# Two linear-attention layers and two MLPs on one core: queries between the entry steps, a fixed TensorE order, eps added by TensorE, the last group scaled on GpSimd, activation tables asked for early

## The chip, the core and the metric

The kernel runs on one core of a Trainium2 chip. A core has TensorE (PE: matrix products, written to PSUM), VectorE (DVE), ScalarE (ACT: functions by table, and copies), GpSimd (POOL) and SyncE (SP), whose queue issues the transfers here. Each engine runs its own instructions in order and waits on semaphores of the others. The metric is the device time of one execution in microseconds (us). In the profile PE stands for matmuls and PEld for the loads of their stationary operand.

## The reference

Input `x` is (1, 2048, 576) in bfloat16. Four residual layers follow each other, A, B, A, B, with the same weights for both A and both B. A is linear attention with 32 heads of 18 columns; B is an MLP of 4608 hidden columns.

```python
def _A_ref(x, wqkv, wo):
    qkv = (x @ wqkv) ...                      # q, k, v: 32 heads of 18
    phi = lambda t: jnp.where(t > 0, t + 1, jnp.exp(t)) + 1e-6
    pq, pk = phi(q), phi(k)
    kv = jnp.einsum("bhsd,bhse->bhde", pk, v)
    z = jnp.einsum("bhsd->bhd", pk)
    num = jnp.einsum("bhqd,bhde->bhqe", pq, kv)
    den = jnp.einsum("bhqd,bhd->bhq", pq, z)[..., None] + 1e-6
    o = num / den
    return o... @ wo
def _B_ref(x, w1, b1, w2, b2):
    y = _layernorm(x, axis=-1)
    h = _gelu(jnp.einsum("bsd,df->bsf", y, w1) + b1)
    return jnp.einsum("bsf,fd->bsd", h, w2) + b2
x = x + _A_ref(_layernorm(x), A_wqkv, A_wo)
x = x + _B_ref(_layernorm(x), B_w1, B_b1, B_w2, B_b2)
# the same two lines once more
```

## The kernel before

**Tiling.** The 2048 tokens are 16 tiles of 128 (`NT`), or four chunks of 512 (`NCA`, `CA`; four tiles a chunk, `TPC`). The 576 columns are five pieces of 128 rows for a product (`KD`), and the 32 heads five groups of 7, 7, 7, 7 and 4 heads (`G`, `GR` rows: 126, or 72 for the last). `yT` holds the normalised input, transposed.

**An attention layer** (`layer_A`; layers 0 and 2). A loop over the 16 tiles makes keys and values (`kv_proj`, L325, L333, L336: key halves in a `ps_h` buffer each, values in a PSUM pair) and adds the tile's outer products to `kvacc` (`kv_acc`, L349). `phi_from_psum` is two ScalarE passes (Exp L278, Identity L280) and two VectorE passes (L281, L283) for each key half or query block. `q_proj(g, c)` (L355) makes the queries of one group and chunk, 126 or 72 rows by 512 tokens, into `pq[(g, c)]`; ten of the twenty stand in this loop.

What I call the entry follows. VectorE masks `kvacc` into `kvT` (L372, L376); five tiny products give `z` (L382), and `zsel` (L384, L386) spreads it. `den_stage(c)` makes the denominators of a chunk for all heads (L409, 20 small matmuls), adds 1e-6 on VectorE (L413), takes the reciprocal (L416) and spreads it into `quad_rden` (L418). `kv_wo(g)` (L394) multiplies a group's key-value matrix by its rows of `wo`; the result is cast from PSUM by ScalarE for even and VectorE for odd groups (L399, L401). `scale_stage(g, c)` brings the reciprocals to the rows of a group (L424), copies them to SBUF on ScalarE (`rden_bc`, L426) and multiplies `pq` by them on VectorE (L427). Before, the next five queries (chunk 2) then come in one block, and `den_stage(1)`.

The output loop over 16 tiles has `wo_stage(t)`: ten matmuls into a PSUM pair (L435; two pairs, `accA` and `accB`, take turns; for each half the groups 0 to 4 in order), `residual` (L305: PSUM plus the old `x`, on VectorE, then a store), and between them the `scale_stage` calls for the next chunk, the last five queries and the other two `den_stage` calls. `prefetch_xo` loads the old `x` of the next tiles with three buffers (L290, L293; for a following MLP with `b2` added on GpSimd, L295). The first four output tiles are normalised at once for the MLP (`LNPipe`: statistics on VectorE, L223 to L231, the root on GpSimd, L236, the normalisation, L248 on ScalarE or L252, and the transposes, L261); later tiles are stored and loaded again (`xl`, L218).

**An MLP layer** (`LayerB`; 1 and 3): per chunk nine groups of four 128-column blocks into PSUM (`m1_group`, L526), Gelu on ScalarE (`hT`, L522; tiny copies `relay_sb`, L531, order the matmuls), and then four tiles of 72 matmuls (L571) and the residual.

**What sets the order.** The program is written for a scheduler that keeps the data dependences and orders each engine's instructions by program order and by its own planned times; it can pull later, ready work ahead, across layers too. An edge of kind `NOSYNC` fixes an order without a semaphore. The helper `pe` chains matmuls that way:

```python
def pe(inst):
    if pe_chain["on"]:
        if pe_chain["last"] is not None:
            tc.add_manual_dep(inst.ins, pe_chain["last"], NOSYNC, reason="TensorE order in the MLP")
        pe_chain["last"] = inst.ins.name
    return inst
```

Before, the chain is on in the MLPs only. The PSUM buffers for short products (`ps_h`) are three, used in turn by keys, queries, `z`, denominators, `rden_ps` and the MLP's `h_ps`. Most SBUF blocks (`pk`, `pq`, `kvwo`, `rden_bc`, `quad_rden`, `hT`) come from one pool, `blk`, of 36.

Of the kernel before, what the change touches and what calls it, by code (L numbers as in the profile page):

```python
# [15 lines left out]
P = 128  # L16
NT = S // P
KD = 5
# [17 lines left out]
def build(tc, A_x, A_wqkv, A_wo, B_w1, B_b1, B_w2, B_b2, out, dbg=None, n_layers=4):  # L36
    nc = tc.nc
    dbg = dbg or {}
    with ExitStack() as ctx:
# [23 lines left out]
        z_row = const.tile([P, 1], BF16, name="z_row")  # L63

        def build_masks():
            sel = nc.gpsimd.affine_select
            nc.gpsimd.memset(maskz[:], 1.0)
            sel(out=maskz[:], in_=maskz[:], compare_op=ALU.is_ge, fill=0.0,
                base=0, pattern=[[-DH, 7], [0, DH]], channel_multiplier=1)
            sel(out=maskz[:], in_=maskz[:], compare_op=ALU.is_ge, fill=0.0,  # L70
                base=DH - 1, pattern=[[DH, 7], [0, DH]], channel_multiplier=-1)
            sel(out=maskz[:], in_=maskz[:], compare_op=ALU.not_equal, fill=1.0,
                base=-126, pattern=[[0, 7], [0, DH]], channel_multiplier=1)
            nc.gpsimd.memset(z_row[:], 0.0)
            sel(out=z_row[:], in_=z_row[:], compare_op=ALU.not_equal, fill=1.0,
                base=-126, pattern=[[0, 1]], channel_multiplier=1)
            nc.gpsimd.memset(head_sel[:], 1.0)
            sel(out=head_sel[:], in_=head_sel[:], compare_op=ALU.is_ge, fill=0.0,
                base=0, pattern=[[126, G], [-DH, H]], channel_multiplier=1)
            sel(out=head_sel[:], in_=head_sel[:], compare_op=ALU.is_ge, fill=0.0,  # L80
                base=DH - 1, pattern=[[-126, G], [DH, H]], channel_multiplier=-1)
            nc.gpsimd.memset(quad_mask[:], 1.0)
            sel(out=quad_mask[:], in_=quad_mask[:], compare_op=ALU.is_ge, fill=0.0,
                base=0, pattern=[[-32, 4], [0, P]], channel_multiplier=1)
            sel(out=quad_mask[:], in_=quad_mask[:], compare_op=ALU.is_ge, fill=0.0,
                base=31, pattern=[[32, 4], [0, P]], channel_multiplier=-1)
            nc.gpsimd.memset(head_bc[:], 0.0)
            hb = head_bc[:, :, 0:126].rearrange("p g (h d) -> p g h d", h=7)
            for quad in range(4):
                sel(out=hb, in_=hb, compare_op=ALU.not_equal, fill=1.0,  # L90
                    base=-32 * quad, pattern=[[-7, G], [-1, 7], [0, DH]], channel_multiplier=1)
# [182 lines left out]
        lnp = LNPipe()  # L274

        def phi_from_psum(ps_ap, out_ap, rows, n):
            e = work.tile([P, 512], BF16, name="phi_e", bufs=3)
            nc.scalar.activation(out=e[0:rows, 0:n], in_=ps_ap, func=ACT.Exp)  # L278
# [34 lines left out]
        def layer_A(li, next_kind, pre_a1=None):  # L313
# [5 lines left out]
            def kv_proj(t):  # L319
                tok = slice(t * P, (t + 1) * P)  # L320
                pk = blk.tile([P, D], BF16, name="pk", tag="blk")
                for half in range(2):
                    kp = ps_h.tile([P, 512], F32, name="k_ps", tag="h")
                    for k in range(KD):
                        nc.tensor.matmul(kp[:, 0:HALF], lhsT=yT[:, k, tok],  # L325
                                         rhs=wqkv_sb[:, k, D + half * HALF: D + (half + 1) * HALF],
                                         start=(k == 0), stop=(k == KD - 1))
# [4 lines left out]
                for k in range(KD):  # L332
                    nc.tensor.matmul(vp[:, 0, 0:252], lhsT=yT[:, k, tok], rhs=wqkv_sb[:, k, 2 * D: 2 * D + 252],  # L333
                                     start=(k == 0), stop=(k == KD - 1))
                for k in range(KD):
                    nc.tensor.matmul(vp[:, 1, 0:324], lhsT=yT[:, k, tok], rhs=wqkv_sb[:, k, 2 * D + 252: 3 * D],  # L336
                                     start=(k == 0), stop=(k == KD - 1))
# [6 lines left out]
            def kv_acc(t):  # L344
                pk = pk_tiles.pop(t)
                va = v_tiles.pop(t)
                for g in range(G):
                    dst = kvacc[:, 0, GO[g]:GO[g] + GR[g]] if g < 4 else kvacc[:, 1, 0:GR[g]]
                    nc.tensor.matmul(dst, lhsT=va[:, g, :], rhs=pk[:, GO[g]:GO[g] + GR[g]],  # L349
                                     start=(t == 0 and g in (0, 4)), stop=(t == NT - 1), skip_group_check=True)  # L350

            def q_proj(g, c):
                qp = ps_h.tile([P, 512], F32, name="q_ps", tag="h")
                for k in range(KD):
                    nc.tensor.matmul(qp[0:GR[g], :], lhsT=wqkv_sb[:, k, GO[g]:GO[g] + GR[g]],  # L355
                                     rhs=yT[:, k, c * CA:(c + 1) * CA],
                                     start=(k == 0), stop=(k == KD - 1))
# [3 lines left out]
            early_q = [(g, c) for c in range(2) for g in range(G)]  # L361
            for t in range(NT):
                if pre_a1 is not None:
                    pre_a1(t)
# [3 lines left out]
                if t >= 4 and early_q:  # L368
                    q_proj(*early_q.pop(0))
            kv_acc(NT - 1)  # L370

# [9 lines left out]
            for g in range(G):  # L381
                nc.tensor.matmul(zp[0:GR[g], g:g + 1], lhsT=kvT[0:127, g, 0:GR[g]], rhs=z_row[0:127, :],  # L382
                                 start=True, stop=True)
# [7 lines left out]
            def kv_wo(g):  # L391
                wp = ps_acc.tile([P, 2, 512], F32, name="kvwo_ps", tag=("accB", "accA")[g % 2])
                for half in range(2):
                    nc.tensor.matmul(wp[0:GR[g], half, 0:HALF], lhsT=kvT[0:GR[g], g, 0:GR[g]],  # L394
                                     rhs=wo_sb[0:GR[g], g, half * HALF:(half + 1) * HALF], start=True, stop=True)
                kvwo[g] = blk.tile([P, D], BF16, name="kvwo", tag="blk")
                out = kvwo[g][0:GR[g], :].rearrange("p (h n) -> p h n", h=2)
                if g % 2:
                    nc.vector.tensor_copy(out=out, in_=wp[0:GR[g], :, 0:HALF])  # L399
                else:  # L400
                    nc.scalar.copy(out=out, in_=wp[0:GR[g], :, 0:HALF])  # L401
# [3 lines left out]
            def den_stage(c):  # L405
                dp = ps_h.tile([P, 512], F32, name="den_ps", tag="h")
                for g in range(G):
                    for j in range(TPC):
                        nc.tensor.matmul(dp[32 * j:32 * (j + 1), 0:P], lhsT=zsel[0:GR[g], g, :],  # L409
                                         rhs=pq[(g, c)][0:GR[g], j * P:(j + 1) * P],  # L410
                                         start=(g == 0), stop=(g == G - 1))
                den = work.tile([P, P], F32, name="den", bufs=1)
                nc.vector.tensor_scalar(out=den[:], in0=dp[:, 0:P], scalar1=1e-6, scalar2=None, op0=ALU.add)  # L413
                rden = work.tile([P, P], BF16, name="rden", bufs=1)
                with nc.allow_low_precision("reciprocal of the denominator in the reference's bfloat16"):
                    nc.vector.reciprocal(out=rden[:], in_=den[:])  # L416
# [5 lines left out]
            def scale_stage(g, c):  # L422
                bp = ps_h.tile([P, 512], F32, name="rden_ps", tag="h")
                nc.tensor.matmul(bp[:], lhsT=head_bc[:, g, :], rhs=quad_rden[c][:, 0:CA], start=True, stop=True)  # L424
                rb = blk.tile([P, D], BF16, name="rden_bc", tag="blk")
                nc.scalar.copy(out=rb[0:GR[g], 0:CA], in_=bp[0:GR[g], :])  # L426
                nc.vector.tensor_tensor(out=pq[(g, c)][0:GR[g], 0:CA], in0=pq[(g, c)][0:GR[g], 0:CA],  # L427
                                        in1=rb[0:GR[g], 0:CA], op=ALU.mult)

            def wo_stage(t):  # L430
                c, j = divmod(t, TPC)
                wp = ps_acc.tile([P, 2, 512], F32, name="wo_ps", tag=("accA", "accB")[t % 2])
                for half in range(2):
                    for g in range(G):
                        mm = nc.tensor.matmul(wp[:, half, 0:HALF], lhsT=pq[(g, c)][0:GR[g], j * P:(j + 1) * P],  # L435
                                              rhs=kvwo[g][0:GR[g], half * HALF:(half + 1) * HALF],
                                              start=(g == 0), stop=(g == G - 1))
                pe_chain["last"] = mm.ins.name
# [3 lines left out]

            den_stage(0)
            for g in range(G):
                kv_wo(g)
            for g in range(G):
                scale_stage(g, 0)
            for g in range(G):
                q_proj(g, 2)
            den_stage(1)  # L450
            late_q = [(g, 3) for g in range(G)]
            for t in range(NT):
# [10 lines left out]
                if late_q and t >= 1:  # L463
                    q_proj(*late_q.pop(0))
                if j == 2 and c + 2 < NCA:
                    den_stage(c + 2)
                lnp.tick()

# [9 lines left out]
        class LayerB:  # L478
# [7 lines left out]
            def m1_group(self, c, g):  # L486
# [32 lines left out]
                def evict(n):  # L519
                    f = g * GF + n  # L520
                    hT[f] = blk.tile([P, D], BF16, name="hT", tag="blk")
                    nc.scalar.activation(out=hT[f][:, 0:CB], in_=dst[n], func=ACT.Gelu_apprx_tanh,  # L522
                                         bias=b1T[:, f:f + 1], scale=1.0)
# [24 lines left out]
            def run(self):  # L548
# [7 lines left out]
                for c in range(NCB):  # L556
# [7 lines left out]
                    self.flush()  # L564
                    hT = self.hT.pop(c)
# [53 lines left out]
        for li, kind in enumerate(kinds):  # L619
# [12 lines left out]
            else:  # L632
                pe_chain["on"] = True
# [50 lines left out]
```

## Time and profile before

| | |
|---|---|
| time, median of 3 runs (lowest, highest) | 822.62 us (822.34, 824.47) |
| the profiled execution's own time | 822.62 us |
| its span, first to last instruction | 820.9 us |
| busy: PE, PEld | 787.6 us (96%), 534.3 us (65%) |
| busy: DVE, ACT, POOL | 265.8 us (32%), 349.3 us (43%), 114.4 us (14%) |
| mean granted TensorE clock | 0.985 |
| moved by DMA | 56.92 MB, mean 69 GB/s |
| layer 0 to layer 3 by first matmul of the next stage | until 131.2, 420.8, 530.5 us, end |

How to read it: busy times are of one execution, and instructions of one engine overlap a little, so that starts matter more than sums. A granted clock of 1.00 is full speed, 0.50 is half. Rows of the windows view give span, then busy time and count of PE, PEld, DVE, ACT and POOL, the clock, the DMA engines' busy share and GB/s. The chain of waits goes back from the last instruction to what released each step; its rows are start, time, what. Timeline rows are start, time, engine, line, operation, and in brackets the idle time before and what ended it.

### The profile page before, as it was taken

The page shows a single profiled execution, that of the slowest core. Times are in us where ns is not written, and L with a number is a line of the kernel's source. Part 1 is how long each engine was busy: PE and PEld are TensorE (multiplying, and loading weights), DVE is VectorE, ACT ScalarE, POOL GpSimd, SP SyncE. Part 2 cuts the span into 40 slices and gives each one's busy share as a digit, 9 for nine tenths or more (in the row PEclk, how much of TensorE's full clock was granted, in tenths as well). Part 3 has the DMA queues.
Part 4 walks back from the last instruction along what each step waited for, and adds up shares of the span by engine and source line. Part 5 has one row for each costly group of instructions (what it writes and reads, how often), then busy time and mean ns, then how long its engine had stood idle before and what let it go on. Part 6 is the DMA issues. An engine that isn't in the chain of part 4 may idle for free.

```text
span 820.9 us, 16092 instructions
## 1 busy us (share of the span) xinstructions
PE 787.6 (96%) x6780; PEld 534.3 (65%) x6780; DVE 265.8 (32%) x782; ACT 349.3 (43%) x758; POOL 114.4 (14%) x209
## 2 busy tenths in 40 slices
PE   5998889999999999999999979899999999999998
PEld 3776556877458647845877756578854774585476
DVE  4675694023303412310345459721400310010000
ACT  4786674710650271066037757275037106403610
POOL 7440031011201201110100001120210110011000
PEclk8999899999999999999999979999999999999999
DMA  9890165001102200100110004920310110011000
GB/s 216 244 320 16 52 215 190 1 30 58 58 16 73 87 2 31 58 30 2 58 59 1 2 1 149 306 95 16 88 44 2 51 51 17 1 45 44 1 23 22
DMA packets 42897, 56.92 MB, mean 69 GB/s; under 512 B 10250, under 2 KB 26890, under 8 KB 42826
## 3 DMA queue, kind: packets, MB, share of 16 engines
q1 hardware_dynamic: 42826, 55.91, 22.3%
q8 instruction: 53, 0.87, 0.4%
q14 instruction: 18, 0.15, 0.1%
HBM read 39.38 MB, written 16.52 MB: 68 GB/s over the span
## 4 chain that ended last, share of the span: by engine, by line
PE 86%; DVE 5%; ACT 2%; DMA 1%; issue 1%; POOL 0%; DVEq 0%; SPq 0%; ACTq 0%
PE m_ps L571 34%; PE h_ps L526 18%; PE hp_ps L526 15%; PE q_ps L355 4%; PE k_ps L325 4%; PE v_ps L336 2%; PE v_ps L333 2%; PE tp L261 2%; DVE xn L305 2%; PE wo_ps L435 1%; PE kvacc L349 1%; PE rden_ps L424 1%; ACT phi_e L278 1%; DVE rden L416 1%; DMA xo<-x_d 1%
## 5 line engine op out<-in xcount | busy, mean ns | idle before, releaser
L571 PE MATMUL m_ps<-w_sb,hT 128*128 128x288 bf16 x2304 | 289.8, 286 | 0.0
L571 PEld LDWEIGHTS <-hT 128*128 128x128 bf16 x2304 | 223.2, 98 | 57.9 <-issue 3.4
L526 PEld LDWEIGHTS <-w_sb 64*128 64x128 bf16 x2304 | 142.9, 94 | 117.1 <-issue 4.3
L526 PE MATMUL hp_ps<-yT,w_sb 64*128 64x512 bf16 x1152 | 173.9, 376 | 0.5 <-DVE xn L305 0.5
L526 PE MATMUL h_ps<-yT,w_sb 64*128 64x512 bf16 x1152 | 152.2, 376 | 0.6 <-ACT hT L522 0.6
L531 ACT COPY relay_sb<-relay_sb 128x1 f32<-128x1 f32 x144 | 28.5, 198 | 279.7 <-PE h_ps L526 236.7
L522 ACT ACTIVATE hT<-h_ps,b1T 128x512 bf16<-128x512 f32 x144 | 91.1, 683 | 43.3 <-PE h_ps L526 43.2
L265 DVE COPY yT<-tp 128x640 bf16<-128x640 bf16 x40 | 19.6, 490 | 269.1 <-PE tp L261 269.0
L522 ACT ACTIVATE hT<-hp_ps,b1T 128x512 bf16<-128x512 f32 x144 | 91.2, 692 | 0.0
L236 POOL TENSOR_TENSOR ln_rstd<-ln_u,neg_half 128x1 f32<-128x1 f32 x64 | 35.5, 556 | 363.8 <-DVE ln_u L229 186.1
L295 POOL TENSOR_TENSOR xo<-xo,b_bc 128x576 f32<-128x576 f32 x32 | 40.9, 1279 | 152.0 <-DMA xo<-x_d 146.2
L435 PE MATMUL wo_ps<-kvwo,pq 126*128 126x288 bf16 (+1 forms) x320 | 46.5, 289 | 8.5 <-DVE xn L305 5.5
L526 PE MATMUL h_ps<-yT,w_tail 64*128 64x512 bf16 x144 | 54.1, 376 | 0.0
L526 PE MATMUL hp_ps<-yT,w_tail 64*128 64x512 bf16 x144 | 54.1, 376 | 0.0
L355 PE MATMUL q_ps<-yT,wqkv_sb 128*126 128x512 bf16 (+1 forms) x200 | 51.5, 397 | 0.0
L435 PEld LDWEIGHTS <-pq 126*128 126x128 bf16 (+1 forms) x320 | 30.2, 98 | 26.1 <-DVE pq L427 9.5
L305 DVE TENSOR_TENSOR xbf<-m_ps,xo 128x576 bf16<-128x576 f32 x16 | 12.1, 758 | 107.4 <-PE m_ps L571 107.4
L325 PE MATMUL k_ps<-wqkv_sb,yT 128*128 128x288 bf16 x320 | 45.9, 291 | 0.0
L278 ACT ACTIVATE phi_e<-k_ps 128x288 bf16<-128x288 f32 x64 | 27.2, 426 | 37.3 <-PE k_ps L325 37.3
L254 POOL COPY y_ring<-y_ring 128x64 bf16<-128x64 bf16 x64 | 16.3, 255 | 161.6 <-DVE y_ring L252 145.5
L281 DVE TENSOR_SCALAR phi_e<-phi_e 128x288 bf16<-128x288 bf16 (+2 forms) x104 | 28.6, 275 | 26.6 <-ACT phi_e L278 26.2
L325 PEld LDWEIGHTS <-yT 128*128 128x128 bf16 x320 | 30.8, 99 | 8.9
(90 smaller groups left out, 667.7 us busy)
## 6 DMA issues: line engine op xcount, KB each, us to landing
x_d<-xn SPq DMA_DIRECT2D x48, 288.0 KB, 2.1
xo<-x_d SPq DMA_DIRECT2D x48, 288.0 KB, 3.0
xl<-x_d SPq DMA_DIRECT2D x24, 288.0 KB, 3.2
w_sb<-in_B_w_dram SPq DMA_DIRECT2D x6, 864.0 KB, 11.0
w_sb<-in_B_w_dram SPq DMA_DIRECT2D x9, 512.0 KB, 4.7
x<-in_A_x_dram SPq DMA_DIRECT2D x16, 144.0 KB, 3.8
xbf<-in_A_x_dram SPq DMA_DIRECT2D x16, 144.0 KB, 3.9
out_dram<-xbf SPq DMA_DIRECT2D x16, 144.0 KB, 1.7
```

The source lines that it names most:

```text
L236: nc.gpsimd.tensor_tensor(out=rstd[:], in0=it["u"][:], in1=neg_half[:], op=ALU.pow)
L278: nc.scalar.activation(out=e[0:rows, 0:n], in_=ps_ap, func=ACT.Exp)
L281: nc.vector.tensor_scalar(out=e[0:rows, 0:n], in0=e[0:rows, 0:n], scalar1=1.0, scalar2=1e-6, op0=ALU.min, op1=ALU.add)
L295: nc.gpsimd.tensor_tensor(out=xo[:], in0=xo[:], in1=b2_bc[:], op=ALU.add)
L305: nc.vector.tensor_tensor(out=xn[:].rearrange("p (h n) -> p h n", h=2), in0=halves, in1=xo[:].rearrange("p (h n) -> p h n", h=2), op=ALU.add)
L325: nc.tensor.matmul(kp[:, 0:HALF], lhsT=yT[:, k, tok], rhs=wqkv_sb[:, k, D + half * HALF: D + (half + 1) * HALF], start=(k == 0), stop=(k = ...
L355: nc.tensor.matmul(qp[0:GR[g], :], lhsT=wqkv_sb[:, k, GO[g]:GO[g] + GR[g]], rhs=yT[:, k, c * CA:(c + 1) * CA], start=(k == 0), stop=(k == ...
L435: mm = nc.tensor.matmul(wp[:, half, 0:HALF], lhsT=pq[(g, c)][0:GR[g], j * P:(j + 1) * P], rhs=kvwo[g][0:GR[g], half * HALF:(half + 1) * HALF],
L522: nc.scalar.activation(out=hT[f][:, 0:CB], in_=dst[n], func=ACT.Gelu_apprx_tanh, bias=b1T[:, f:f + 1], scale=1.0)
L526: mm = pe(nc.tensor.matmul(dst[n], lhsT=wt, rhs=mv, start=(seen[n] == 0), stop=(seen[n] == 8)))
L531: relay = nc.scalar.copy(out=relay_sb[:, 1:2], in_=relay_sb[:, 0:1])
L571: pe(nc.tensor.matmul(acc[:, half, 0:HALF], lhsT=hT[f][:, j * P:(j + 1) * P], rhs=w2_sb[:, f, half * HALF:(half + 1) * HALF], start=(f == ...
```

## The change

Six edits, the first two in one stroke. (1) `pe` is put around all matmuls of the attention layers, and the chain is on from the second half of the key loop in layer 0, and all through layer 2: TensorE's order there is the program's. (2) The twenty query projections are one list, `q_left`: twelve in the key loop (tiles 4 to 15), six between the entry steps, two in the output loop; the entry steps are interleaved by hand. (3) The 1e-6 of the denominator is added by four one-row matmuls per `den_stage`, and the reciprocal reads PSUM. (4) All five `kvwo` casts are on ScalarE. (5) The product of the last group with `rden_bc` is on GpSimd in chunks 1 to 3. (6) A dummy activation asks for the Gelu table late in the output loop, not before the last Exp, and one for the Exp table after the last Gelu.

```diff
+        eps_row = const.tile([1, H], BF16, name="eps_row")
+        one_row = const.tile([1, P], BF16, name="one_row")
+        act_dummy = const.tile([P, 1], F32, name="act_dummy")
...
+        def warm_table(func, after):
+            warm = nc.scalar.activation(out=act_dummy[:, 0:1], in_=neg_half[:, 0:1], func=func)
+            tc.add_manual_dep(warm.ins, after, NOSYNC, reason="table of the next stage loaded early")
...
-            early_q = [(g, c) for c in range(2) for g in range(G)]
+            q_left = [(g, c) for c in range(NCA) for g in range(G)]
+            pe_chain.update(on=(li > 0), last=None)
             for t in range(NT):
+                if t == NT // 2:
+                    pe_chain["on"] = True
...
-                if t >= 4 and early_q:
-                    q_proj(*early_q.pop(0))
+                if t >= 4:
+                    q_proj(*q_left.pop(0))
+            q_proj(*q_left.pop(0))
             kv_acc(NT - 1)
+            q_proj(*q_left.pop(0))
...
-                if g % 2:
-                    nc.vector.tensor_copy(out=out, in_=wp[0:GR[g], :, 0:HALF])
-                else:
-                    nc.scalar.copy(out=out, in_=wp[0:GR[g], :, 0:HALF])
+                nc.scalar.copy(out=out, in_=wp[0:GR[g], :, 0:HALF])
...
-                                         start=(g == 0), stop=(g == G - 1))
-                den = work.tile([P, P], F32, name="den", bufs=1)
-                nc.vector.tensor_scalar(out=den[:], in0=dp[:, 0:P], scalar1=1e-6, scalar2=None, op0=ALU.add)
+                                         start=(g == 0), stop=False))
+                for j in range(TPC):
+                    pe(nc.tensor.matmul(dp[32 * j:32 * (j + 1), 0:P], lhsT=eps_row[:], rhs=one_row[:],
+                                        start=False, stop=True))
...
-                    nc.vector.reciprocal(out=rden[:], in_=den[:])
+                    nc.vector.reciprocal(out=rden[:], in_=dp[:, 0:P])
...
-                nc.vector.tensor_tensor(out=pq[(g, c)][0:GR[g], 0:CA], in0=pq[(g, c)][0:GR[g], 0:CA],
+                eng = nc.gpsimd if c > 0 and g == G - 1 else nc.vector
+                eng.tensor_tensor(out=pq[(g, c)][0:GR[g], 0:CA], in0=pq[(g, c)][0:GR[g], 0:CA],
                                         in1=rb[0:GR[g], 0:CA], op=ALU.mult)
...
+            kv_wo(0)
+            q_proj(*q_left.pop(0))
             den_stage(0)
-            for g in range(G):
-                kv_wo(g)
-            for g in range(G):
+            q_proj(*q_left.pop(0))
+            kv_wo(1)
+            den_stage(1)
+            for g in range(3):
                 scale_stage(g, 0)
-            for g in range(G):
-                q_proj(g, 2)
-            den_stage(1)
-            late_q = [(g, 3) for g in range(G)]
+            kv_wo(2)
+            q_proj(*q_left.pop(0))
+            for g in range(3, G):
+                scale_stage(g, 0)
+            kv_wo(3)
+            kv_wo(4)
+            q_proj(*q_left.pop(0))
...
-                if late_q and t >= 1:
-                    q_proj(*late_q.pop(0))
+                if q_left:
+                    q_proj(*q_left.pop(0))
                 if j == 2 and c + 2 < NCA:
                     den_stage(c + 2)
+                if t == NT - 3:
+                    warm_table(ACT.Gelu_apprx_tanh, act_last["exp"])
                 lnp.tick()
+            pe_chain["on"] = False
...
                     self.flush()
+                    if c == NCB - 1 and next_kind == "A":
+                        warm_table(ACT.Exp, act_last["gelu"])
```

## Prediction

> **What bounds the kernel now.** The page first: the span in 40 slices of 20.5 us. TensorE (PE) is full nearly everywhere; its granted clock falls only in the first slice, in the fifth and in the 24th.
>
> ```profile
> PE   5998889999999999999999979899999999999998
> DVE  4675694023303412310345459721400310010000
> PEclk8999899999999999999999979999999999999999
> ```
>
> The fifth slice holds the second half of layer 0 (attention), slices 24 to 26 that of layer 2. The two MLPs run at full share and are not touched. So I cut both attention tails with the windows view: entry (from the last key projection to the first whole output tile), then four chunks of four output tiles, c0 to c3. Columns: span, then busy us and count of PE, PE weight loads, VectorE (DVE), ScalarE (ACT), GpSimd (POOL), then clock, DMA share, GB/s.
>
> ```profile
> 75.06:95.18 20.12, 15.73 (x122) 9.68 (x120) 10.78 (x29) 11.45 (x23) 0.00 (x0) 0.83 0.00 1
> 95.18:105.39 10.21, 9.71 (x85) 6.28 (x78) 9.96 (x29) 5.88 (x12) 2.77 (x3) 1.00 0.56 177
> 105.39:116.84 11.45, 10.16 (x97) 6.96 (x96) 11.24 (x30) 9.69 (x18) 4.87 (x8) 1.00 0.52 159
> 116.84:124.39 7.55, 6.34 (x48) 4.29 (x46) 6.09 (x16) 3.23 (x6) 0.55 (x1) 1.00 0.87 280
> 124.39:131.23 6.84, 5.37 (x42) 3.70 (x41) 5.16 (x14) 0.58 (x1) 1.02 (x3) 1.00 0.92 294
> ```
>
> Three limits follow each other. The entry has no full engine: PE is idle 4.4 us and slow. c0 and c1 belong to DVE (9.96 of 10.21, 11.24 of 11.45). c2 and c3 have DMA at 0.87 to 0.92. In layer 2 the same five take 20.88, 10.21, 10.29, 7.93 and 7.55.
>
> The chain of waits through layer 0's entry shows why nothing is full: one PE step, one DVE step, one PE step.
>
> ```profile
> 77.71 0.59 ACT v_ring L338
> 78.86 0.69 DVE kvT L372
> 81.22 0.30 DVE den L413
> 81.54 0.96 DVE rden L416
> 82.53 0.44 DVE quad_rden L418
> 85.75 0.59 ACT rden_bc L426
> 88.18 3.46 PE q_ps L355 x10
> ```
>
> In PE's timeline these are idle times of 0.41 (L338), 0.78 (L372), 1.84 (L418) and 1.25 us (L426). Windows of half a microsecond show the granted clock at 0.50 from 83.7 to 90.6, and from 479.8 to 490.0 in layer 2. The ten query matmuls of 88.18 take 3.46 us; a projection of five takes 1.08 to 1.10 elsewhere.
>
> **Part 1: queries between the entry steps.** No query work is added or removed: 20 projections a layer, as before. Today 10 lie in the key loop, 5 in a block before the loop, 5 in the loop. After: 12 in the key loop, 6 between the entry steps, 2 in the loop. I lay PE's new order out from the key projection of tile 15, at full-clock pitches of the chain: K and V of one tile 2.46, accumulation 0.26, query 1.08, kvwo pair 0.25, den 0.40 to 0.48, rden_ps 0.22.
> - PE: 2.46 + 2 x 0.26 + 7 queries 7.58 + z 0.3 + 5 kvwo 1.25 + 2 den 0.96 + 5 rden_ps 1.1 = 14.2 us. One more query, 1.08, goes ahead of it at tile 14: 15.3.
> - ACT: four key passes at 0.305 and V 0.58 make 1.8; seven queries at 1.08 (two passes of 0.59, overlapping) 7.6; five kvwo at 0.55 2.75; five rden_bc at 0.52 2.6: 14.8 us. It is as full as PE, in order, and frees the three ps_h buffers.
>
> Stepping both queues with those three buffers, the holds that remain are the third rden_ps (its buffer is freed by the second reciprocal), the last query (a buffer freed by ACT) and the first output tile (fifth rden_bc, then pq, and the last kvwo): together about 1.8 us. Whole entry about 17.1 us against 20.12 and 20.88: minus 3.0 and minus 3.8. Bounds: 15.3 (minus 4.8 and 5.6) and, if ACT's order is bad and the clock still falls, no gain. The waits for kvT, zsel and the first quad_rden (0.78, 0.3, 1.84) each get a query of 1.08 or more behind which they hide; should such a query be held by its buffer, they return in full.
>
> The clock is part of this. About 5.7 us of layer 0's and 7.3 us of layer 2's matmuls run at half rate, with no idle stretch over 1.84 us but a busy share under one half in the 4 us before. In my order PE is busy 0.9 of the time, and the rows with 0.81 and more stand at 1.00. [...]
>
> **Part 2: the fixed order itself.** In layer 2's key loop PE already runs in program order (K, V, accumulation, query, step of 3.81 us without idle): 0. Two queries more there are PE work moved, and ACT has 3.4 of 3.81 us a step: 0.
>
> **Part 3: DVE in c0 and c1.** Gone from these 21.66 us (20.50 in layer 2): the chain of den(1), now in the entry, 0.28 + 0.94 + 0.41 = 1.63; the eps additions of den(2) and den(3), 2 x 0.28; three of six query pairs at 0.29 + 0.42, 2.13; two last-group products, 1.10 + 0.41 (layer 2: 0.40 + 0.41). Sum 5.83 and 5.13. DVE instructions overlap by about 0.08 each, 13 of them 1.04: minus 4.8 and minus 4.1. PE's floor for c0 and c1 is 8 x 1.235 + 10 x 0.22 + 2 x 1.08 + 2 x 0.48 + 4 transposes x 0.28 = 16.3, so PE does not cut this short. The eps matmuls, four a den at den's 0.02 each, are 0.65 us over the whole kernel on PE, beside DVE work: 0. A reciprocal that reads PSUM isn't in the trace; the 128x128 read from PSUM is 0.28 in all, so I bound it by 0 and plus 0.28, and take 0. The two kvwo casts (0.75) move from DVE to ACT in the entry, counted there.
>
> **Part 4: last group on GpSimd.** Three times a layer the next chunk starts with rden_ps, ACT 0.58, product, then the fifth wo matmul. No product stands on POOL in the trace; the nearest row is the 128x576 add of L295, 1.28 us, or 2.22 ns an element: 512 of them 1.14. With hops 1.8 us, of which four wo matmuls cover 0.5: PE stands 1.3. Today it stands at the same places 1.09, 0.18, 1.05, and 0.31, 0.17, 1.18, mean 0.66. Net plus 0.6, six times: plus 3.6. From below 0 (where DVE is late anyway); from above plus 1.9 each, if an add of L295 stands ahead in POOL's order, as three do in layer 0 at 103.9 to 110.4:
>
> ```profile
> 105.75 1.27 POOL L295 TENSOR_TENSOR xo<-xo,b_bc 128x576 f32<-128x576 f32 x1 [0.49 <-DMA xo<-x_d]
> 106.20 1.10 DVE L427 TENSOR_TENSOR pq<-pq,rden_bc 72x512 bf16<-72x512 bf16 x1
> 109.48 1.24 DVE L427 TENSOR_TENSOR pq<-pq,rden_bc 126x512 bf16<-126x512 bf16 x1
> ```
>
> A DVE product that meets a POOL add lasts until that add ends (1.10 and 1.24 for 0.41). Behind the new POOL product DVE's next work is mostly xn, from PSUM, which such rows do not lengthen; I leave it inside the bound. [...]
>
> **Part 5: tables.** The Exp load of layer 2 already runs at 385.84, right after the last Gelu and 35 us before its use: 0. The Gelu loads stand on the path, 1.28 us each, but PE then waits only 0.18 and 0.37: minus 0.5. If a load came between queries, ACT has room in c1 (9.7 of 11.45 with five queries in c0 and c1, two after).
>
> **Sum.** The profiled execution took 822.62 us, 1.7 around its span of 820.9; it is also the median of the runs. Minus 3.0, 3.8, 4.8, 4.1 and 0.5, plus 3.6: minus 12.6, so 810.0.
>
> **Rivals.**
> - Given back to transfers, 816. c2 and c3 run at DMA 0.87 to 0.93, xn waited for its xbf load three times (1.2 us) and for xo 1.55 in layer 2, with three buffers and 3.4 us to landing. If c2 and c3 go from 1.8 to 2.05 us a tile (plus 4 us in both layers) and 2 us of c0 and c1 are lost too, 6 return. For: the share. Against: c0 and c1 leave DMA near half free. 0.24.
> - PE alone is the bound, 800. Entry at 15.3 (minus 10.4), c0 and c1 at 16.3 (minus 9.6), c2 and c3 minus 1 each layer, tables 0.5: minus 22.5. Against: ACT as full as PE in the entry, the GpSimd hop. 0.12.
> - Slower, 826. DVE and the SP queue are in order, and normalisation work of the next MLP stands among the xn additions: the chain shows the store of a tile 3.68, its reload 3.70, and DVE waiting 1.24 for it while xn queues behind. With TensorE's order fixed, other engines' order is planned anew; if all four reloads of each layer stand ahead of xn and hold it 2.0 us more than now, plus 16. From 1.6 us each it eats the gain. Against: of the first three in layer 0 only one waits now. 0.10.
> - The change does nothing that counts (the early Exp table, part 2): within 2.5 us. It would need the entry to stay as it is and c0 and c1 to be held by the hop. 0.04.
>
> The forecast's own case, 804 to 815, has 0.50. The range from 802 to 818 takes in most of the transfer rival and cuts the floor case in half. A measurement here can tell about 0.3% (2.5 us) from no change: faster by more 0.86, within 0.04, slower 0.10.
>
> **What would show it.** Right: entry windows near 17 us at a clock over 0.95; DVE busy about 17 us in c0 and c1; rden_ps not waiting for quad_rden; PE waiting about 1.3 us for the POOL product at each chunk start; no table load after relay_sb; c2 and c3 as now. Wrong: a clock of 0.5 in the entry again; POOL products over 1.5 us; DVE idle behind xl or xo; c2 plus c3 over 16 us.

## The result, and the profile after

The changed kernel takes **813.48 us** (median of four runs, 810.53 to 816.66) against 823.55 us for the kernel before, run beside it (822.34 to 824.91): ratio 0.9878, 95% interval 0.9836 to 0.992. It is faster by 10.1 us; forecast were 12.6 and the time 810.0. The profiled execution is the longest of the four, 816.66 us (span 814.7, mean clock 0.989), so the profiled pair differs by only 6.0 us; the shortest run, 810.53, has a mean clock of 0.994. Terms below are first read in the profiled pair and then held against the medians.

The page's slices of after: only the first slice keeps a clock below 9. PE is full now in the fourth, fifth and 24th slice; the dips that are left stand in the sixth (7, before 8) and in 25 and 26 (8 and 7, before 9 and 8), which hold the output loops.

```profile
PE   5999979999999999999999998799999999999998
DVE  4675873024303502310345468621400310010000
PEclk8999999999999999999999999999999999999999
```

The windows of layer 0, cut as before: the entry (from the last key projection to the first whole output tile) and the chunks c0 to c3 of four output tiles. Columns as before.

```profile
75.44:91.58 16.14, 15.28 (x134) 9.69 (x133) 11.04 (x32) 13.94 (x29) 0.00 (x0) 1.00 0.00 1
91.58:100.47 8.89, 8.83 (x79) 5.92 (x80) 7.71 (x24) 7.55 (x14) 2.39 (x3) 1.00 0.45 137
100.47:112.38 11.91, 9.61 (x89) 6.51 (x89) 9.64 (x23) 7.46 (x13) 5.71 (x10) 0.86 0.69 207
112.38:120.85 8.47, 6.46 (x47) 4.30 (x46) 6.32 (x16) 3.40 (x6) 1.93 (x3) 1.00 0.79 253
120.85:129.04 8.19, 5.73 (x43) 3.76 (x43) 6.35 (x17) 0.58 (x1) 2.67 (x5) 1.00 0.77 253
```

The entry is full (15.28 of 16.14) at full clock. c0 has turned from VectorE's to TensorE's (8.83 of 8.89; VectorE 7.71). c1 is longer than before (11.91 for 11.45, at a mean clock of 0.86), and c2 and c3 too (16.66 for 14.39), at a lower share of the DMA engines (0.79 and 0.77 for 0.87 and 0.92). In layer 2 the five are 16.14, 8.89, 11.91, 8.82 and 8.78; its last chunk, too, has a clock below 1.00 (0.81). Summed, the four chunks take 37.46 and 38.40 us, where they took 36.05 and 35.98.

What TensorE waits for in the output loop, from its timeline: at each chunk's start the product that now stands on GpSimd.

```profile
103.44 1.62 PE L450 MATMUL wo_ps<-kvwo,pq 72*128 72x288 bf16 x6 [1.91 <-POOL pq L442]
114.22 0.91 PE L450 MATMUL wo_ps<-kvwo,pq 72*128 72x288 bf16 x6 [1.18 <-POOL pq L442]
122.76 2.33 PE L450 MATMUL wo_ps<-kvwo,pq 72*128 72x288 bf16 x16 [1.26 <-POOL pq L442]
```

With layer 2 (1.90, 1.19, 1.92) that is 9.4 us; before, the same six places cost 4.0. Why the first is so long is seen on ScalarE's timeline: ahead of the last group's copy (the row of 101.59) stand the Gelu table, asked for "late" but run right behind the last Exp, and two normalisation passes.

```profile
98.19 1.28 ACT L284 ACT_TABLE_LOAD   x1
99.49 0.20 ACT L284 ACTIVATE act_dummy<-neg_half 128x1 f32<-128x1 f32 x1
99.60 0.57 ACT L440 CAST rden_bc<-rden_ps 126x512 bf16<-126x512 f32 x1
100.06 1.63 ACT L254 ACTIVATE y_ring<-xn,ln_nmr,ln_rstd 128x576 bf16<-128x576 f32 x2
101.59 0.57 ACT L440 CAST rden_bc<-rden_ps 72x512 bf16<-72x512 f32 x1
```

The chain of waits shows what else stands in c2 and c3: the MLP's reload `xl` and the old `x`.

```profile
102.24 1.15 POOL pq L442
106.77 1.76 DVE pq L442 x2
110.12 4.18 DMA xl<-x_d
118.14 4.63 DMA xbf<-in_A_x_dram
```

VectorE's timeline has the wait itself: statistics of a reload for the next layer, with xn additions of this one queued behind.

```profile
114.33 0.46 DVE L229 BATCH_NORM_STATS2 ln_st<-xl 128x6 f32<-128x288 f32 x1 [1.39 <-DMA xl<-x_d]
122.89 0.76 DVE L316 TENSOR_TENSOR xn<-wo_ps,xbf 128x576 f32<-128x576 f32 x1 [1.32 <-DMA xbf<-in_A_x_dram]
```

### The profile page after: what moved, and what is told of

Same layout as the page of the kernel before. It is cut to its first block, busy times and chain, and to the rows that moved or that the text cites. A ratio compares the mean times of both kernels' runs of the same rounds, so it can differ in the third digit from the quotient of the medians.

```text
span 814.7 us, 16146 instructions
## 1 busy us (share of the span) xinstructions
PE 785.2 (96%) x6806; PEld 510.1 (63%) x6812; DVE 259.2 (32%) x764; ACT 352.2 (43%) x765; POOL 120.6 (15%) x218
## 4 chain that ended last, share of the span: by engine, by line
PE 88%; DVE 3%; ACT 3%; DMA 2%; POOL 1%; issue 1%; SPq 0%; DVEq 0%; ACTq 0%
PE m_ps L596 35%; PE h_ps L549 19%; PE hp_ps L549 15%; PE q_ps L366 5%; PE k_ps L336 4%; PE v_ps L347 2%; PE wo_ps L450 2%; PE v_ps L344 2%; PE tp L267 2%; DMA xl<-x_d 1%; PE kvacc L360 1%; DVE xn L316 1%; ACT rden_bc L440 1%; DMA xbf<-in_A_x_dram 1%; POOL ln_rstd L242 1%
## 5 line engine op out<-in xcount | busy, mean ns | idle before, releaser
L549 PEld LDWEIGHTS <-w_sb 64*128 64x128 bf16 x2304 | 124.4, 94 | 136.5 <-issue 1.7
L549 PE MATMUL hp_ps<-yT,w_sb 64*128 64x512 bf16 x1152 | 178.0, 376 | 0.0
L549 PE MATMUL h_ps<-yT,w_sb 64*128 64x512 bf16 x1152 | 147.9, 376 | 0.0
L450 PE MATMUL wo_ps<-kvwo,pq 126*128 126x288 bf16 (+1 forms) x320 | 49.3, 301 | 13.5 <-POOL pq L442 9.4
L549 PEld LDWEIGHTS <-w_tail 64*128 64x128 bf16 x288 | 27.1, 94 | 17.1
```

The source lines that it names most:

```text
L450: pe(nc.tensor.matmul(wp[:, half, 0:HALF], lhsT=pq[(g, c)][0:GR[g], j * P:(j + 1) * P], rhs=kvwo[g][0:GR[g], half * HALF:(half + 1) * HALF ...
L549: mm = pe(nc.tensor.matmul(dst[n], lhsT=wt, rhs=mv, start=(seen[n] == 0), stop=(seen[n] == 8)))
```

## The experiments

Each was compared with the kernel before, run beside it in the same set (medians 823.36, 824.97 and 823.04 us). The change itself stands at 0.9878 (0.9836 to 0.992).

| run | edit | us | ratio (95%) |
|---|---|---|---|
| e4_order_alone | before, with edits 1 and 2 only | 814.92 | 0.9884 (0.9861 to 0.9907) |
| h3_order_free | change, chain of matmuls off | 813.47 | 0.9871 (0.9842 to 0.99) |
| e3_pool_alone | before, with edit 5 only | 827.37 | 1.0045 (1.0028 to 1.0061) |
| e1_last_on_dve | change without edit 5 | 818.49 | 0.9936 (0.9913 to 0.996) |
| e2_no_gelu_warm | change without the Gelu request | 814.56 | 0.9891 (0.9869 to 0.9914) |
| h4_eps_on_vector | change without edit 3 | 810.96 | 0.9849 (0.9822 to 0.9877) |
| g1_scale_earlier | change, scaling called a tile earlier | 810.19 | 0.9827 (0.9813 to 0.984) |
| g2_reloads_held | change, MLP's reloads held | 807.76 | 0.9805 (0.9787 to 0.9822) |
| g3_dve_and_held | g2 without edit 5 | 807.42 | 0.979 (0.9772 to 0.9807) |
| h2_hold_on_before | before, MLP's reloads held | 818.08 | 0.9942 (0.9915 to 0.9968) |
| g4_three_together | g2, g1 and a later Gelu request | 805.62 | 0.9773 (0.9758 to 0.9789) |
| h1_three_on_dve | g4 without edit 5 | 804.36 | 0.9775 (0.9742 to 0.9808) |

**e4_order_alone: is it the order of queries and entry?** The kernel before with `q_left`, the entry steps interleaved and the chain on; eps, casts, product and tables as before.

```diff
-            early_q = [(g, c) for c in range(2) for g in range(G)]
+            q_left = [(g, c) for c in range(NCA) for g in range(G)]
+            pe_chain.update(on=(li > 0), last=None)
...
+            kv_wo(0)
+            q_proj(*q_left.pop(0))
             den_stage(0)
...
```

> The kernel before with the order part alone: queries between the entry steps and the fixed TensorE order; eps on VectorE, kvwo casts split, products on VectorE, no early tables. Prediction's terms: minus 6.8 for the entry, and of the VectorE term the moved denominator chain and queries, 3.76 a layer less overlap, minus 6.4: 809 to 811. Transfer theory: the entry's 6.8 alone, 815 to 817. If the entry needs the eps and cast edits as well, its windows stay over 18 us.

Measured 814.92: 8.4 of the 10 us, and above the 809 to 811 of the prediction's terms. In the profiled pair the entries give 7.3 of it, with the moved queries given back, and the four chunks take 36.57 and 35.90 us, as much as before: VectorE's relief, which was to bring 6.4, brought next to nothing. The other four edits together are worth some 1.5 us, within what the intervals can't tell from nothing. From the last key projection to the first whole output tile it takes 15.77 us, less than the change's 16.14 (both from the first matmul of the one to that of the other).

**h3_order_free: is it the chain, or the program's order?** `pe_chain` stays off in the attention layers (the last output matmul is still named, so that the MLP's chain begins behind it); everything else is the change.

```diff
-            pe_chain.update(on=(li > 0), last=None)
+            pe_chain.update(on=False, last=None)
...
```

> The change with the chain of matmuls switched off in the attention layers: the scheduler orders TensorE by its own times again; queries, eps, GpSimd product and tables as in the change. Part 2 of the prediction (the fixed order itself is worth 0, only the program order that it holds counts): 811 to 816 us. Rival (without the chain the scheduler pulls queries together again or lets the entry steps wait): 817 to 822, with entry windows of 18 us and more and the clock at 0.5 in them.

Measured 813.47, the same as the change. The window of its entry:

```profile
75.64:91.72 16.08, 15.46 (x137) 9.83 (x135) 11.07 (x32) 13.96 (x29) 0.00 (x0) 1.00 0.00 1
```

Part 2 holds: where the queries and the entry steps stand in the program is worth 8 us, and forbidding the scheduler to move them nothing that these runs can tell. In the output loop its waits sit elsewhere, 1.98 us for an xn addition in layer 0 and 2.42 in layer 2, and 0.37 to 0.56 for GpSimd.

**e3_pool_alone: what does the GpSimd product do by itself?** The kernel before with one line changed.

```diff
-                nc.vector.tensor_tensor(out=pq[(g, c)][0:GR[g], 0:CA], ...
+                eng = nc.gpsimd if c > 0 and g == G - 1 else nc.vector
+                eng.tensor_tensor(out=pq[(g, c)][0:GR[g], 0:CA], ...
```

> The kernel before with one part of the change alone: the last group's product on GpSimd in chunks 1 to 3. Hop theory: 4 to 7 us slower than before, 827 to 830, with waits of 1.2 us or more at each chunk start. Prediction's term: plus 3.6, 826. If VectorE is what holds the first two chunks and transfers the others, the product's place matters little: 821 to 824.

Measured 827.37: 4.0 slower, beside Part 4's plus 3.6. GpSimd's timeline shows the upper bound that Part 4 named, two additions of L295 ahead of the product:

```profile
102.20 1.49 POOL L295 TENSOR_TENSOR xo<-xo,b_bc 128x576 f32<-128x576 f32 x1
104.06 1.27 POOL L295 TENSOR_TENSOR xo<-xo,b_bc 128x576 f32<-128x576 f32 x1 [0.37 <-DMA xo<-x_d]
105.29 1.15 POOL L428 TENSOR_TENSOR pq<-pq,rden_bc 72x512 bf16<-72x512 bf16 x1
```

TensorE then waits 2.03 us for it, and a VectorE pass that meets the product takes 0.94 us (the first `phi_e` pass at 105.65) instead of 0.29. The window of c1:

```profile
103.81:118.07 14.26, 12.05 (x96) 7.62 (x95) 10.79 (x30) 9.71 (x17) 5.82 (x9) 0.88 0.55 173
```

It is 2.8 us longer than before (11.45), 1.9 of it TensorE's busy time at a lower clock. The size agrees with Part 4, its mechanism does not: TensorE's rows name the product only three times (2.03, 0.30 and 0.49 us), and the first expectation's waits of 1.2 us at each chunk start aren't there. Lost are one long wait, the half clock behind it and, later in the loop, waits for xn additions (1.98 us at one place of layer 2); that the price came out near 3.6 is luck.

**e1_last_on_dve: is the product a loss in the change too?** The change, with `eng = nc.vector`.

```diff
-                eng = nc.gpsimd if c > 0 and g == G - 1 else nc.vector
+                eng = nc.vector
```

> The change with one part undone: the last group's product back on VectorE in all chunks. Hop theory (the output loop gave back its gain at the three chunk starts, where TensorE waits 1.2 to 1.9 us for the GpSimd product, and at the half clock that follows the longest of them): the waits there, 9.4 us over both layers, fall to about 4, the clock in the second chunk is back at 1.00, and the time is 806 to 809. Transfer theory (the loop is held by loads and by reloads queued ahead of the additions): the last two chunks stay above 16 us and the time at 812 to 815.

Measured 818.49: 5 us slower than the change (the two intervals just overlap), against both expectations. Alone the edit loses 4; within the change, undoing it loses 5. On VectorE the product now comes behind a statistic that waits for its reload:

```profile
114.48 0.46 DVE L229 BATCH_NORM_STATS2 ln_st<-xl 128x6 f32<-128x288 f32 x1 [0.62 <-DMA xl<-x_d]
114.85 0.40 DVE L442 TENSOR_TENSOR pq<-pq,rden_bc 72x512 bf16<-72x512 bf16 x1
```

and TensorE waits 1.68 us for that product at 115.31, 2.42 at the same place of layer 2 (1.18 and 1.19 in the change). So I took GpSimd's product for a way round a blocked VectorE queue, and tried that next. These rows alone don't show it: the six chunk-start waits sum to 9.4 us, as in the change, and 1.8 of the 3.1 us between the two profiled executions lie in the MLP of layer 1, whose start runs at half clock from 128.27 to 135.09.

**g2_reloads_held: what do the reloads cost?** The MLP's `xl` loads come behind the attention layer's last store in SyncE's queue, and their first statistic behind its last addition in VectorE's; an order is fixed, and no wait added.

```diff
+                        ld = nc.sync.dma_start(out=xn[:], in_=x_d[it["load"]])
+                        if a_end["st"] is not None:
+                            tc.add_manual_dep(ld.ins, a_end["st"], NOSYNC, reason="...")
...
+                        if it["load"] is not None and a_end["xn"] is not None:
+                            tc.add_manual_dep(bn.ins, a_end["xn"], NOSYNC, reason="...")
...
+            if li % 2 == 0 and t == NT - 1:
+                a_end.update(xn=add.ins.name, st=st.ins.name)
```

> The change, with the next MLP's reloads of output tiles and their statistics ordered behind the attention layer's last store and addition on their own engines (order edges alone, no new semaphore). Queue theory: the waits for a reload (1.4 us in layer 0, 1.75 in layer 2) and what they hold go, the last two chunks fall from 16.7 and 17.6 to about 14 us, and the time to 808 to 810. Chunk-start theory: the waits for the GpSimd product remain and the gain is under 2: 811.5 to 813.5. A loss would mean that the MLP needs these reloads early.

Measured 807.76, 5.7 us under the change. Its windows for c0 to c3 of layer 0:

```profile
91.80:100.68 8.88, 8.82 (x78) 5.92 (x79) 7.70 (x24) 7.54 (x14) 2.38 (x3) 1.00 0.44 137
100.68:111.26 10.58, 8.16 (x90) 5.71 (x89) 9.17 (x22) 7.24 (x13) 6.01 (x10) 1.00 0.71 221
111.26:118.64 7.38, 6.14 (x48) 4.30 (x47) 4.84 (x10) 3.39 (x6) 1.15 (x1) 1.00 0.74 235
118.64:125.24 6.60, 5.20 (x42) 3.71 (x41) 3.00 (x4) 0.58 (x1) 1.15 (x1) 1.00 0.71 240
```

c2 and c3 take 13.98 instead of 16.66 us (and 13.98 instead of 17.60 in layer 2), and no xn addition holds TensorE there any more. The DMA share falls with the time (0.74 and 0.71, where it was 0.79 and 0.77): it had not been the transfers' rate. The six waits for GpSimd's product stay (9.0 us in all). c1 is 1.33 us shorter with TensorE's busy time 1.45 less at a clock of 1.00 (0.86 in the change): that is the clock, on which more below. It is as much in layer 2, together 2.7 of the 8.9 us between the two profiled executions; how much of the medians' 5.7 us is the clock, no run tells.

**g3_dve_and_held and h1_three_on_dve: is GpSimd of use once the way is free?** g3 is g2 with `eng = nc.vector`; h1 is g4 (below) with the same line.

> The last group's product on VectorE in all chunks, and the reloads held as in the run before. If GpSimd was of use only because its queue is free while VectorE's stands behind a reload, then with the reloads gone VectorE does as well: the same as the held run with GpSimd within 2 us, and about 8 us faster than with VectorE and reloads (818.5). If VectorE's own work in the first two chunks is what makes its product late, it stays 3 us or more slower than the held run with GpSimd.

> g4_three_together with the last group's product back on VectorE. Theory A (GpSimd's product only goes round a VectorE queue that stands behind the reloads; with the reloads held it buys and costs nothing, as g3 against g2): 804 to 808 us, within 2 of g4's 805.6, chunk-start waits on VectorE's product under 1 us. Rival B (the product is a relief of its own for VectorE, which is full when the scaling is called earlier): 808 to 811, xn waits growing by more than the chunk-start waits shrink. Rival C (the hop over GpSimd costs 0.5 us at each of six chunk starts even here): 801 to 803.

Measured 807.42 beside 807.76, and 804.36 beside 805.62: no difference in either pair. With the reloads held, the product costs and brings nothing.

**h2_hold_on_before: did the change bring the reloads' cost?** The hold of g2, put into the kernel before.

> The kernel before with nothing but the hold: the MLP's reload (xl) and its first statistics come after the attention layer's last store and last addition. Theory A (the reloads cost in any order of TensorE, since VectorE's and SyncE's queues are in order): 818 to 821 us, minus 3 to 6 against before. Rival B (before, VectorE is behind with its own work in c0 and c1, and the reloads come only where transfers are the limit, so that the hold moves little): 822 to 825. If B, the reloads' cost is one that the fixed order brought or made visible, and the hold is worth its 5.7 us only behind it.

Measured 818.08: 5.0 us less than before (by its interval 0.32% to 0.85%), beside 5.7 behind the change. The reloads cost both kernels about the same. That corrects what I had made of g2: they explain why both kernels stay above what their engines need, and perhaps why edit 5 looks useful, but not by themselves why the change brought less than its sum. Its windows for c2 and c3 together, layer 0 and layer 2:

```profile
116.83:128.81 11.98, 11.55 (x89) 8.00 (x87) 8.04 (x15) 3.81 (x7) 0.00 (x0) 1.00 0.77 253
512.43:526.42 13.99, 11.70 (x88) 8.07 (x87) 8.22 (x15) 3.81 (x7) 0.00 (x0) 1.00 0.91 296
```

**g1_scale_earlier and e2_no_gelu_warm: the wait at the chunk start.** In g1 the last group of the next chunk is scaled one output tile earlier; in e2 the Gelu request is left out.

```diff
-                    for g in ((0, 1), (2,), (3,), (4,))[j]:
+                    for g in ((0, 1), (2, 3), (4,), ())[j]:
```

> The change, with the scaling of the next chunk's groups one output tile earlier: groups 2 and 3 after the second tile, group 4 after the third (before: 2, 3, 4 after the second, third, fourth). The work is the same. Chunk-start theory (what the output loop gave back are the waits of 1.2 to 1.9 us for the last product, 9.4 us over both layers, and the half clock after them): the waits go, minus 6 to 9: 804.5 to 807.5. Queue theory (reloads of later tiles stand among the additions on VectorE and in the transfer queue): the last two chunks stay at 16 us or more and the gain is 0 to 3: 810.5 to 813.5.

> The change without the early request for the Gelu table (the one for Exp stays). Table theory (the load of 1.28 us stands on ScalarE ahead of the copy that the first chunk start waits for): the first wait of each layer falls from 1.9 us to about 0.8, the half clock behind it may go, at the cost of up to 0.9 us at each MLP start: 810 to 812. If the load is hidden in the loop: 813 to 815, and the first wait stays at 1.9.

g1 measured 810.19, 3.3 us under the change at the medians, with intervals that just overlap; that is the edge of its queue theory's range and far from that of the chunk starts. In the profiles the six waits for GpSimd shrink from 9.4 to 1.7 us in all. Layer 0's two that are left, and two others of its loop:

```profile
101.38 0.91 PE L450 MATMUL wo_ps<-kvwo,pq 72*128 72x288 bf16 x6 [0.81 <-POOL pq L442]
118.83 2.37 PE L450 MATMUL wo_ps<-kvwo,pq 72*128 72x288 bf16 x16 [0.18 <-POOL pq L442]
121.89 1.39 PE L450 MATMUL wo_ps<-kvwo,pq 126*128 126x288 bf16 x10 [0.69 <-DVE xn L316]
124.23 1.39 PE L450 MATMUL wo_ps<-kvwo,pq 126*128 126x288 bf16 x10 [0.95 <-DVE xn L316]
```

More than half of these 7.7 us is given back, in part to waits for xn additions as in the last two rows (2.30 us at one place of layer 2). e2 measured 814.56, not to be told from the change: the first wait falls from 1.91 to 1.36 us, a new one of 1.36 for a `yT` copy on ScalarE stands behind it, and the table load is back at the MLP's start. By these rows Part 5's gain is spent in the second chunk.

**h4_eps_on_vector: edit 3 undone.** The 1e-6 is added by VectorE again.

```diff
-                for j in range(TPC):
-                    pe(nc.tensor.matmul(dp[32 * j:32 * (j + 1), 0:P], lhsT=eps_row[:], rhs=one_row[:],
-                                        start=False, stop=True))
+                den = work.tile([P, P], F32, name="den", bufs=1)
+                nc.vector.tensor_scalar(out=den[:], in0=dp[:, 0:P], scalar1=1e-6, scalar2=None, op0=ALU.add)
...
```

> The change with 1e-6 added by VectorE again, by one instruction of 0.28 us in each of eight denominators, and without the four one-row matmuls. Part 3 of the prediction (0.56 us of VectorE a layer in c0 and c1 and a longer first chain in the entry, both only partly on the path): 813.5 to 816 us. Rival A (the second step in the reciprocal's chain delays the first scaling and with it the first output tile fully): 816 to 818. Rival B (the matmuls cost as much as they save): 812 to 813.5.

Measured 810.96: against all three expectations, not slower but 2.5 us under the change, with overlapping intervals. That edit 3 costs 2.5 us is therefore not shown; that it brings nothing is likely. Between the same two matmuls as in e4 the entry is 15.88 us, 0.26 shorter than the change's. TensorE's timeline of the change has the price of the four one-row matmuls, from their start to the next:

```profile
98.84 0.23 PE L426 MATMUL den_ps<-one_row,eps_row 1*32 1x128 bf16 x4
99.00 1.41 PE L450 MATMUL wo_ps<-kvwo,pq 126*128 126x288 bf16 x10
```

That is 0.16 us a denominator and 1.3 for all eight, twice Part 3's 0.65, and the two in the entry make up its 0.26.

**g4_three_together: the version that the runs point to.** The change with the hold of g2, the earlier scaling of g1, and the Gelu request behind the last `rden_bc` copy, so that the table loads at 117.50 us and not at 98.

> The change with scaling one tile earlier, reloads held, and the Gelu request ordered behind the last reciprocal copy. If both theories hold a part, the gains add: 801 to 805, with the output loop under 33 us in each layer (37.5 and 38.4 in the change). If one of them carries it all, it equals the better of the two single runs within 2 us.

Measured 805.62, 7.9 us under the change, with intervals apart; h1, the same with all products on VectorE, 804.36. Both beat both kernels; between the two the runs do not decide.

## Why the forecast was right, and where its sum was not

**Part 1, the entry: right in size and cause.** Forecast were 17.1 us, the extra query at tile 14 among them, and so 16.0 without it; measured 16.14 us in both layers, clock 1.00. With the 1.08 of the moved query given back, the gain is 2.90 and 3.66 us, forecast 3.0 and 3.8. `rden_ps` no longer waits for `quad_rden`. e4 shows it without the other edits.

**Part 2: right.** h3 runs as fast without the chain.

**Part 3, VectorE's relief in c0 and c1: the step that failed.** The relief came: VectorE is busy 17.35 us there in layer 0 instead of 21.20, 3.85 less (forecast 4.8; products that meet a GpSimd addition take up part of the rest, 1.76 us for two at 106.77 against 0.75 for two at 117.66; an xn addition that meets GpSimd's product keeps its time, 0.73 us at 101.84). But the time fell by 0.86 us, and rose by 0.30 in layer 2. The sum took 4.8 off today's time and added a net 0.6 for the hop, which gives 17.46; "so PE does not cut this short" rested on a floor of 16.3. Once VectorE no longer sets the pace, the stretch is TensorE's work plus TensorE's own waits, and both were larger. g2's windows give the work at full clock, 8.82 + 8.16 = 16.98. After, TensorE is busy 8.83 + 9.61 = 18.44, so half clock costs 1.46; idle are 20.80 - 18.44 = 2.36, of which 1.91 are the one wait for GpSimd. Against 17.46 that is 0.7 of floor (0.3 of it the eps matmuls of two denominators, put at 0), 1.5 of clock and 1.2 of idle time. The step should have been made from the next bound, not as a difference to the old one. The rows of before had it: TensorE's 9.71 + 10.16 us in c0 and c1, less the three queries of 1.08 that leave them, are 16.6, and in layer 2 it was the fuller engine of c1 already (9.98 us, VectorE 9.73):

```profile
504.69:514.98 10.29, 9.98 (x97) 6.90 (x96) 9.73 (x30) 9.61 (x18) 2.25 (x6) 1.00 0.64 202
```

**Part 4, the GpSimd product: price right, place wrong.** The product takes 1.15 us (forecast 1.14, from the rate of a row with another shape), 2.9 times VectorE's 0.40. TensorE's six waits sum to 9.4 instead of 7.8 us, net plus 5.4 instead of plus 3.6. The excess is in waits of 1.9 us, which at the first chunk start of layer 0 is ScalarE's order: the copy that feeds the product stands behind a table load and two normalisation passes. That the edit loses 4 us alone was foreseen, if not the way in which e3 lost them; that taking it out of the change loses 5 was not, since the sum gave each edit one price whatever stands around it.

**Part 5: small either way.** No table load follows `relay_sb` any more (they stand at 98.19, 383.03 and 494.15 us); e2 shows that the total does not feel it.

**The rivals.** "Given back to transfers" named 816 for c2 and c3 growing by 2 us a layer. They grew by 2.27 and 2.12 (16.66 and 17.60 us, over the 16 set as a sign of being wrong), but not by the DMA share that was the argument for it: the share fell. "c2 and c3 as now" among the signs of being right did not even fit the sum, which had Part 4's plus 0.6 at both chunk starts. What grew shows when the reloads are held in both kernels. In layer 0 the two chunks then take 13.98 us (g2) against 11.98 (h2): 2.0 of the 2.27 stay, and in TensorE's rows there are waits of 1.18 and 1.40 us for GpSimd's product against one of 0.18 for VectorE's. In layer 2 they take 13.98 against 13.99: the growth goes with the hold, and some 1.1 us of it had been half clock in the last chunk (TensorE busy 6.86 us there, 5.73 in layer 0). So the mechanism of the "slower" rival, reloads for the next MLP among the xn additions, has at most a part in the growth: VectorE waits 1.39 us for one in layer 0 and 1.75 in layer 2, far from the 2.0 us for each of four that would have eaten the gain. g2 and h2 show that holding the reloads is worth 5 to 6 us in either kernel: most of what that rival feared stood in the kernel before already.

Of the medians' 10.1 us, the entry accounts for 6.6 and everything else for 3.5, where 5.8 were forecast. That rest does not stand where the sum had it. In the profiled pair the chunks c0 to c3 are 1.4 and 2.4 us longer, where Parts 3 and 4 together had minus 5.3 for both layers; outside entry and chunks, where the sum had minus 0.5, 3.5 us are gone (0.7 and 0.5 from the key loops, the moved query given back, 0.6 and 1.7 from the MLPs), and no run takes these apart. So the total came near 810 in part by luck. The profiled execution has 3.2 us more than its median; half clock in three places of its output loops (1.45 us in c1 of layer 0, as much in layer 2, 1.1 in layer 2's last chunk) would cover that, but no profile of a shorter run of the change is on record.

**What stays open.** The sizes of edits 3 and 4 one by one lie under what these runs can tell. From e4 to the change there are 1.4 us, of which edit 5 would be 5 and the others a loss of 3.6: e1 is e4 with edits 3, 4 and 6, and their intervals lie apart. h4 and the entry's 15.77, 15.88 and 16.14 us point the same way, but edit 4 (all `kvwo` casts on ScalarE) was not run by itself.

## What to carry to other kernels

When a change relieves the engine that sets the pace, sum the stretch anew from the next engine's work and its waits at that engine's queue order; a difference to the old time credits relief that nobody can use. An edit that moves work to a slower engine (here 1.15 us on GpSimd for 0.40 on VectorE) may only be a detour round a blocked in-order queue: look for what blocks it (here loads of the next layer and their statistics, pulled ahead by the scheduler) and hold that back first. Price an edit in the company it will have, since by the medians the same line cost 4 us, saved 5 and did nothing in three surroundings.

## What the runs showed of the hardware

**The clock.** Behind the first slice, TensorE of the change falls to half clock at 103.40, 499.35 and 519.83 us, each time for 3.41 us; in the kernel before, the two stretches at half clock last 6.83 us (83.82 to 90.65) and 10.24 us (479.77 to 490.01).

The change and g2 have the same wait of 1.91 us for GpSimd's product, the change from 101.53 to 103.44 and g2 from 101.74 to 103.65. The rows of g2:

```profile
99.13:102.54 3.41, 2.38 (x19) 1.40 (x19) 3.41 (x8) 3.23 (x6) 2.22 (x5) 1.00 0.68 206
102.54:105.96 3.42, 2.31 (x20) 1.75 (x21) 2.31 (x9) 1.57 (x3) 3.29 (x5) 1.00 0.81 228
```

and of the change:

```profile
99.99:103.40 3.41, 1.30 (x9) 0.58 (x6) 3.41 (x10) 2.17 (x4) 2.21 (x5) 1.00 0.72 219
103.40:106.82 3.42, 3.38 (x16) 2.12 (x17) 1.42 (x7) 2.16 (x4) 2.71 (x5) 0.50 0.74 228
```

In the change TensorE is busy for 1.30 of the 3.41 us ahead of the fall, and the row behind it stands at half clock. The rows of g2 are taken over other stretches around the same wait; TensorE is busy for 2.38 and 2.31 us in them, and the clock stays at 1.00. So a wait of 1.9 us was followed by half clock in one run, with 1.45 us more of TensorE's busy time in c1, and not in the other. The busy share does not tell when: before, 476.35 to 479.77 is busy for 2.05 us and half clock follows, 524.14 to 527.55 for 1.79 us and the clock stays at 1.00. The prediction's reading, a share under one half in the 4 us before, therefore fits layer 0 (2.05 of 4.00 us) only nearly and layer 2 (2.63) not at all. What makes the clock fall, these runs do not show.

**Operand from PSUM.** The reciprocal takes 0.94 to 0.95 us from PSUM as from SBUF; of the bounds of 0 and plus 0.28, the lower holds.
